# Summing w_out from its bf16 tile instead of its f32 load buffers, in a fused attention and MLP kernel

## The chip, the cores and the metric

The kernel runs on one core of a Trainium2 chip. The metric is device time in microseconds of one launch, as the median of several runs. A core has a tensor engine (PE) for matrix products, a vector engine (DVE), a scalar engine for activations (ACT), a general engine (POOL), and a sync engine (SP), which here issues nearly all the transfers (DMA). Each engine works through its own list of instructions in order; engines wait for each other by semaphores. A profile of one execution stands beside the times.

## The reference

Attention with 4 sequences, 8 heads, 768 tokens and 64 elements a head, each query seeing the 8 first keys and the 96 latest ones, with a distance bias; then softplus between two weight products.

```python
scores = scale * np.matmul(q, k.transpose(0, 1, 3, 2))
...
scores = scores + bias[None, :, :, :]
scores = np.where(keep, scores, -1000000000.0)
...
a = a / (np.sum(a, axis=-1, keepdims=True) + 1e-09)
return np.matmul(a, v).astype(np.float32)
...
h = x @ w_in
g = np.maximum(h, 0.0) + np.log1p(np.exp(-np.abs(h)))
return (g @ w_out).astype(np.float32)
```

x is the attention's output with its heads put side by side (3072 tokens of 512). w_in is 512 x 2048, w_out 2048 x 512.

## The kernel before, in words

**Tiling.** The 3072 tokens are 24 blocks of 128 (numbered n = 0 to 23 in the order of `UNITS`), two blocks a load unit (i = 0 to 11) and two blocks a group (g = 0 to 11) for the weight products.

**One block's attention.** q, k and v of a unit are loaded in f32 (`ldq`, `ldk`, `ldv`, lines 598 to 644, 512 KB each) into a ring of 14 buffers called raw; cast to bf16 (`castq`, `castk`, `castv`); q and k are transposed, from unit 3 on by DMA (`trq`, `trk`, lines 853 to 868). Then scores on PE (`sc`, line 980), bias added on DVE (`z`, line 1006), exponentials on ACT (`ex`, line 1013), the weighted values on PE (`pv`, line 1032), the normalizing on DVE (`nm`, lines 1043 and 1044), and a transpose to the tile XT (`xt`, line 1075, by DMA). The copies `gk` and `gv` bring the 8 global keys and values into the rows that the block before no longer needs, so they wait for that block's `pv`.

**One group's weight products.** `a{g}.{p}` is the first product in eight parts of eight matmuls (line 1227), `e` the exponential (line 1255) and `ln` the logarithm (line 1265) that make softplus; the result is the tile g. For groups 0 and 1 the second product is dense: `b{g}.{half}.{x}` (line 1286), two matmuls of 512 columns each, then a copy `oc` and a store. From group 2 on the second product is made by seven block products instead of eight (Strassen): `b{g}.{j}`, j from 1 to 7, eight matmuls of 256 columns each (line 544). Five of them multiply with sums or differences of quarters of w_out, and five with differences of quarters of g (`ka`, line 468). `oe` puts the products together in the output tile (lines 499 to 527). Groups 10 and 11 make the first product by seven block products too (`kw`, `kx`, `mA` to `mD`, `mt`, `md`, `eo`, `ed`).

**w_out and its sums.** `wout0` to `wout7` (line 669) load 256 rows each, 512 KB, into raw buffers. `cout0` to `cout7` (line 673) cast them into the bf16 tile `w_out_bf`, which groups 0 and 1 and the products 2 and 5 use. `weight_sums` (lines 409 to 441) makes twenty sums of 128 x 512, `ws{p}.{j}` (line 430): for each p from 0 to 3 and each j of 6, 1, 4, 3, 7, from the rows of `wout{2p}` (X) and `wout{2p+1}` (Y); j = 6 needs X alone and j = 7 needs Y alone. They go to DVE or POOL, in bf16, into raw buffers that have become free (`homes`, among them those of w_out 0, 1 and 2). The buffers of w_out 3, 4 and 5 return to the ring at the end of `weight_sums`, and by the ring's order they are the next homes of `ldk4`, `ldv4` and `ldq5`.

**The order.** All steps stand in one list, `ORDER`, written out by hand, each with its engine (P for PE, V for DVE, A for ACT, G for POOL, S for SP); each engine issues its steps in the order of the list. A step's waits follow from what it reads and writes (`Program.op`, lines 28 to 54). Loads from unit 3 on are also gated by a part of the first product (lines 1517 to 1521), so that they do not come too early: for `ldk3` that is `a0.4`. Up to some 28 us PE also has 35 fillers (`fill`, line 1414), products of a blank tile that keep its clock up.

```python
op(f"ws{p}.{j}", "DVE", 0.0, rank, ex, reads={"6": xk, "7": yk}.get(j, xk + yk), writes=[("W", j, p)],
   port=True, after=[u for key in raw_keys(slot, (part // 2,)) for u in users(key)],
   alts={"DVE": 0.66, "POOL": 1.3})
...
for slot in (at[6], at[7]):
...
idle.extend((at[3], at[4], at[5]))
```

Of the kernel before, what the change touches and what calls it, by code (L numbers as in the profile page):

```python
# [85 lines left out]
castq2.1:V a0.3:P e0.0:A gk8:G ldv2:S castk2.1:V xt2:P ln0.0:A trq2.0:P xc2:V trk2.0:P e0.3:A wout3:S cin5:V pv3.0:P  # L86
fill32:P cpk2.1:A a0.2:P nm3.0:V cin4:V fill33:P e0.2:A pv3.1:P fill34:P cpq2.1:V a0.5:P gv8.1:G ln0.1:A cpk2.0:V
nm3.1:V cin6:G a0.4:P e0.5:A cpq2.0:V wout4:S xt3:P e0.4:A cin7:V sc4.0:P xc3:V ln0.2:A a0.7:P wout5:S z4.0:V cout0:G
a0.6:P e0.7:A z4.1:V ldq3:S b0.0.0:P e0.6:A cout1:G a1.1:P ws0.4:V ex4.1:A ldk3:S a1.0:P ws0.3:V e1.1:A b0.0.2:P
cout2:V e1.0:A a1.3:P wout7:S ex4.0:A ws0.1:V castv2.00:G a1.2:P castv2.01:V ln1.0:A gk5:G b0.0.4:P ws0.6:V pv4.0:P  # L90
e1.2:A sc5.0:P ws1.4:V e1.3:A b1.0.0:P nm4.0:V cout3:A b1.0.2:P ws2.6:G a1.5:P z5.0:V ln0.3:A pv4.1:P wout6:S cout4:G
b0.0.6:P nm4.1:V ldv3:S sc5.1:P e1.5:A gv5.0:V a1.4:P cout5:A castv2.10:G z5.1:V castv2.11:G xt4:P castq3.0:A a1.7:P
ws1.7:V gv5.1:G ws1.1:V b0.1.0:P e1.4:A trq3:S b0.1.2:P ln1.1:A b0.1.4:P ws0.7:V b0.0.8:P xc4:A castk3.0:V b0.1.6:P
ex5.0:A a1.6:P ws2.7:V ws1.3:V e1.7:A ldq4:S b0.1.8:P cout6:V ex5.1:A b0.1.10:P trk3.0:S b0.0.10:P cout7:V b1.0.4:P
e1.6:A ws2.1:V pv5.0:P gk6:A b0.1.12:P ln1.2:A ldk4:S nm5.0:V b0.0.12:P trk3.1:S ws2.4:V b0.0.14:P pv5.1:P ws2.3:V
oc0.0.0:A b0.1.14:P gv6.0:G b1.0.6:P ln1.3:A nm5.1:V b1.0.8:P ldv4:S oc0.1.0:V castv3.11:G b1.0.10:P castq4.0:A
gv6.1:V xt5:P castv3.00:G sc6.0:P xc5:V castv3.10:A castv3.01:G trq4:S b1.0.12:P z6.0:V b1.0.14:P ws1.6:G a2.1:P
oc1.0.0:A ldq5:S z6.1:V ex6.0:A a2.0:P castk4.0:G ex6.1:A pv6.0:P b1.1.0:P trk4.0:S nm6.0:V b1.1.2:P e2.0:A gk7:V
pv6.1:P ws3.3:V e2.1:A sc7.0:P gv7.1:G nm6.1:V ln2.0:A ldk5:S a2.2:P z7.0:V gv7.0:G xt6:S a2.3:P castv4.10:G e2.2:A
z7.1:V ex7.0:A ws3.4:G b1.1.4:P b1.1.6:P trk4.1:S e2.3:A gv8.0:V b1.1.8:P castq5.0:G pv7.0:P ex7.1:A sc8.0:P nm7.0:V  # L100
st0.0.0:S a2.5:P ln2.1:A z8.0:V trq5:S castv4.01:G castv4.11:G pv7.1:P e2.5:A b1.1.10:P nm7.1:V castv4.00:G a2.4:P
ex8.0:A z8.1:V xt7:S a2.7:P e2.4:A ws3.6:V ex8.1:A st0.1.0:S pv8.0:P b1.1.12:P nm8.0:V ldv5:S a2.6:P e2.7:A ldq6:S
ws3.7:V gk9:G ln2.2:A b1.1.14:P pv8.1:P castk5.0:G oc1.1.0:V sc9.0:P e2.6:A ws3.1:V a3.1:P ln2.3:A trk5.0:S gv9.1:G
z9.0:V a3.0:P e3.1:A gv9.0:G ldk6:S b2.3:P z9.1:V ka2.6:G e3.0:A ex9.0:A b2.4:P nm8.1:V ex9.1:A ka2.7:V a3.2:P xt8:S
pv9.0:P e3.2:A gk10:G a3.3:P nm9.0:V ldv6:S oe2.a:A trk5.1:S ka2.2:V a3.4:P e3.3:A ka2.1:V ln3.0:A pv9.1:P sc10.0:P
nm9.1:V gv10.0:G e3.4:A a3.5:P z10.1:V xt9:S castq6.0:G b2.1:P e3.5:A ka2.5:V ldq7:S ex10.1:A a3.6:P oe2.1:V trq6:S
gv10.1:V a3.7:P z10.0:V gk11:G e3.6:A castv5.00:G ln3.1:A b2.5:P castv5.01:G castk6.0:V st1.0.0:S e3.7:A b2.2:P
castv6.01:G ldk7:S ex10.0:A trk6.0:S sc11.0:P oe2.c:V castv5.11:G a4.0:P z11.1:V castq7.0:G trk6.1:S pv10.0:P e4.0:A
b2.7:P nm10.0:V ln3.3:A castv5.10:G z11.0:V a4.2:P trq7:S castv6.11:G ln3.2:A pv10.1:P a4.1:P st1.1.0:S gv11.0:G
e4.2:A ka3.6:V b2.6:P gv11.1:G e4.1:A nm10.1:V ex11.0:A a4.4:P ka3.2:V castv6.00:G xt10:S oe2.7:V a4.3:P e4.4:A  # L110
castk7.0:G ldv7:S sc12.0:P e4.3:A pv11.0:P z12.1:V b3.3:P trk7.0:S ka3.1:G ex11.1:A nm11.0:V a4.5:P ln4.0:A z12.0:V
pv11.1:P e4.5:A a4.6:P nm11.1:V ex12.0:A castv6.10:V xt11:S b3.4:P ex12.1:A ka3.7:V e4.6:A a4.7:P ka3.5:G oe3.a:V
ln4.1:A st2.0.0:S sc13.0:P ldq8:S e4.7:A ldv9:S pv12.0:P z13.1:V b3.1:P ln4.3:A ldk8:S a5.0:P castv7.00:V ex13.1:A
oe3.1:V a5.1:P ldv8:S z13.0:V castv7.01:A gk14:G b3.5:P e5.0:A nm12.0:V e5.1:A b3.2:P ex13.0:A trk7.1:S castq8.0:G
sc14.0:P oe3.c:V ln4.2:A castv7.11:G pv12.1:P a5.2:P nm12.1:V castv9.00:G ln5.0:A z14.1:V a5.3:P castv7.10:G xt12:S
pv13.0:P castv9.10:G castv9.11:V e5.3:A b3.7:P castk8.0:G ex14.1:A st2.1.0:S nm13.0:V b3.6:P ka4.1:V gk15:A trk8.0:S
a5.5:P e5.2:A castv8.11:G oe3.7:V ln5.1:A pv13.1:P castv8.01:G a5.4:P st3.0.0:S nm13.1:V gv14.1:G z14.0:V xt13:S
b4.3:P e5.4:A e5.5:A b4.4:P ka4.7:V ldq9:S ln5.2:A ka4.5:V a5.6:P trq8:S castv9.01:V gv14.0:A a5.7:P ka4.6:V oe4.a:A
st3.1.0:S kw1.1:V e5.6:A ka4.2:G sc15.0:P e5.7:A b4.1:P ex14.0:A a6.0:P trk8.1:S oe4.1:V z15.1:V a6.1:P e6.0:A ldk9:S
ln5.3:A pv14.0:P ldv10:S b4.5:P nm14.0:V castq9.0:G ex15.1:A z15.0:V b4.2:P ldk11:S ka5.6:G gk16:A pv14.1:P e6.1:A  # L120
oe4.c:V a6.2:P trq9:S ex15.0:A nm14.1:V sc16.0:P gv15.1:A a6.3:P gv15.0:G z16.0:V castk9.0:G b4.7:P e6.3:A z16.1:V
e6.2:A pv15.0:P castv8.00:G trk9.1:S b4.6:P ln6.0:A nm15.0:V castv8.10:G a6.5:P oe4.7:V ex16.1:A castv10.10:G ka5.1:V
a6.4:P st4.0.0:S ex16.0:A xt14:S pv15.1:P b5.3:P gk17:A gv16.1:V e6.5:A gv16.0:V nm15.1:V ldq10:S b5.4:P ka5.2:V
trk9.0:S pv16.0:P ka5.7:V oe5.a:A sc17.0:P nm16.0:V e6.4:A xt15:S ka5.5:G b5.1:P z17.0:V ln6.2:A pv16.1:P a6.6:P
st4.1.0:S gv17.1:A oe5.1:V ldv11:S a6.7:P gv17.0:V e6.6:A nm16.1:V ex17.0:A z17.1:V b5.5:P xt16:S castk11.0:G e6.7:A
b5.2:P ldk10:S ln6.3:A pv17.0:P oe5.c:V sc18.0:P ln6.1:A a7.1:P z18.1:V castq10.0:V a7.0:P ex18.1:A nm17.0:V e7.1:A
b5.7:P z18.0:V e7.0:A ex18.0:A b5.6:P ka6.1:V ex17.1:A a7.2:P castk10.0:G oe5.7:V ka6.7:V sc19.0:P st5.0.0:S e7.2:A
castv10.11:G st5.1.0:S a7.3:P ln7.0:A z19.0:V trq10:S ka6.5:G pv17.1:P e7.3:A b6.3:P nm17.1:V ex19.0:A trk10.0:S
z19.1:V a7.4:P castv11.11:G pv18.0:P xt17:S b6.4:P e7.4:A nm18.0:V castv10.00:G kw1.0:V a7.5:P oe6.a:A castv11.10:G
trk10.1:S pv18.1:P a7.6:P e7.5:A nm18.1:V castv10.01:G ex19.1:A kw5.0:V b6.1:P ldq11:S e7.6:A a7.7:P gk20:G oe6.1:V  # L130
ka6.6:V a8.0:P e7.7:A ka6.2:V ln7.3:A pv19.0:P a8.1:P nm19.0:V ln7.1:A kw5.1:V b6.5:P kw7.0:V e8.0:A pv19.1:P kw7.1:V
b6.2:P e8.1:A castv11.01:V ln7.2:A a8.2:P oe6.c:V sc20.0:P e8.2:A ka7.6:G a8.3:P ln8.0:A z20.1:V b6.7:P e8.3:A
nm19.1:V ex20.1:A castv11.00:G a8.4:P z20.0:V xt19:S gv20.1:G b6.6:P gk21:A e8.4:A ka7.2:V gv20.0:G xt18:S ex20.0:A
a8.5:P oe6.7:V castq11.0:G ka7.7:V sc21.0:P st6.1.0:S e8.5:A trk11.0:S a8.6:P ln8.1:A z21.0:V ka7.5:G pv20.0:P e8.6:A
b7.3:P st6.0.0:S trk11.1:S nm20.0:V ex21.0:A a8.7:P z21.1:V b7.4:P trq11:S e8.7:A kw2.0:V ex21.1:A a9.0:P ka7.1:V
pv20.1:P oe7.a:V gk22:G e9.0:A a9.1:P gv21.1:G nm20.1:V ln8.2:A b7.1:P kw6.1:V xt20:S e9.1:A gv21.0:V a9.2:P oe7.1:V
ln8.3:A kw6.0:V pv21.0:P sc22.0:P e9.2:A ka8.6:G nm21.0:V ln9.0:A a9.3:P z22.1:V pv21.1:P e9.3:A a9.4:P z22.0:V
ex22.1:A gv22.1:G b7.5:P gv22.0:V e9.4:A nm21.1:V a9.5:P ex22.0:A gk23:V xt21:S ka8.2:V b7.2:P e9.5:A kw2.1:V ln9.1:A
sc23.0:P oe7.c:V a9.6:P z23.0:V ln9.2:A kx10.1:G a9.7:P e9.6:A z23.1:V kx10.3:G pv22.0:P e9.7:A b7.7:P kx10.7:G
nm22.0:V ln9.3:A kx10.4:G mA10.0:P ka8.1:V b7.6:P kx10.6:G my10.0:A mA10.1:P oe7.7:V mA10.3:P my10.1:A mA10.2:P  # L140
pv22.1:P my10.2:A mB10.0:P st7.0.0:S nm22.1:V ex23.0:A gv23.0:G mB10.1:P st7.1.0:S mt10.0:V mB10.2:P gv23.1:G xt22:S
ex23.1:A b8.3:P mt10.1:V ka8.7:G pv23.0:P mC10.0:P nm23.0:V b8.4:P mt10.2:V eo10.0:A ka8.5:G pv23.1:P oe8.a:A mC10.1:P
nm23.1:V mD10.0:P eo10.1:A xt23:S b8.1:P md10.0:V mC10.2:P my10.3:A ka9.6:G oe8.1:V mD10.1:P eo10.2:A mB10.3:P b8.5:P
# [1431 lines left out]
```

## Time and profile before

| what | us |
|---|---|
| median of 3 runs (lowest, highest) | 210.27 (209.87, 211.12) |
| the profiled execution's own time | 210.3 |
| its span, from the first to the last instruction | 208.5 |
| PE busy | 200.5 |
| DVE busy | 175.5 |
| ACT busy | 165.9 |
| POOL busy | 109.2 |

Busy time is a sum over the whole span; it does not say which engine sets the end. For that the profile follows the chain that ended last, back from the last instruction: at each step to what released it, or to the instruction before it on its engine. PE has 93% of that chain. A group of instructions is shown as line, engine, operation, tiles and shapes, then its count, busy time, mean time of one in ns, and the idle time ahead of it with what ended it. A timeline row is its start, its duration, the engine, the line and the tiles. The granted clock was 0.998 of the full one.

### The profile page before, as it was taken

The numbers are of one execution on the slowest core, as the hardware profiler recorded it, in microseconds if no ns is written. First come the engines' busy times: TensorE is split into PE (matmuls) and PEld (weight loads), VectorE is DVE, ScalarE is ACT, GpSimd is POOL, SyncE is SP. The second block draws the span as 40 slices with busy tenths as digits, with TensorE's granted clock in tenths as the row PEclk, the third lists the DMA queues.
The fourth block names the chain that finished last, engine by engine and source line by source line (L and its number), as shares of the span: only waits on it lengthen the run. The fifth ranks groups of instructions, "written<-read, shape, count | busy, mean of one in ns | idle before, by whom it ended". The sixth has DMA issues, their size and how long they took to land.

```text
span 208.5 us, 5775 instructions
## 1 busy us (share of the span) xinstructions
PE 200.5 (96%) x2307; PEld 165.0 (79%) x2307; DVE 175.5 (84%) x330; ACT 165.9 (80%) x245; POOL 109.2 (52%) x130
## 2 busy tenths in 40 slices
...
GB/s 174 364 360 389 386 356 362 335 236 266 190 250 214 245 207 306 200 177 305 215 198 271 219 220 214 186 145 0 119 161 14 16 129 28 101 3 101 0 63 143
DMA packets 70650, 41.00 MB, mean 197 GB/s; under 512 B 30432, under 2 KB 62688, under 8 KB 70624
## 3 DMA queue, kind: packets, MB, share of 16 engines
...
q10 hardware_dynamic: 688, 0.66, 1.0%
...
## 4 chain that ended last, share of the span: by engine, by line
PE 93%; DMA 3%; DVE 1%; ACTq 0%; ACT 0%; POOL 0%; issue 0%; DVEq 0%
PE h_ps L1227 34%; PE o_ps L544 27%; PE s_ps L980 6%; PE x_ps L1032 5%; PE o_ps L1286 3%; PE s_ps L1286 3%; PE h_ps L1167 3%; DMA raw<-in_q_dram 3%; PE s_ps L1167 3%; PE x_ps L1414 2%; PE s_ps L544 1%; PE s_ps L840 1%; PE x_ps L544 1%; PE o_ps L1032 1%; PE s_ps L961 1%; PE s_ps L820 0%
## 5 line engine op out<-in xcount | busy, mean ns | idle before, releaser
L1227 PE MATMUL h_ps<-XT,w_in_bf 128*128 128x256 bf16 x640 | 79.6, 273 | 0.0
L1227 PEld LDWEIGHTS <-w_in_bf 128*128 128x128 bf16 x640 | 60.5, 98 | 9.8
L1255 ACT ACTIVATE e<-h_ps 128x512 f32<-128x512 f32 x80 | 50.1, 640 | 9.3 <-PE h_ps L1227 8.8
L1006 DVE TENSOR_TENSOR z<-s_ps,biasA 128x1024 f32<-128x1024 f32 x38 | 45.6, 1216 | 1.9 <-PE s_ps L980 1.9
L1013 ACT ACTIVATE pb<-z 128x1024 bf16<-128x1024 f32 (+1 forms) x44 | 43.1, 992 | 0.7 <-DVE rcp L1043 0.4
L1265 ACT ACTIVATE g<-e 128x1024 bf16<-128x1024 f32 x40 | 41.7, 1054 | 0.4
L544 PEld LDWEIGHTS <-g 128*128 128x128 bf16 x320 | 30.6, 98 | 3.8 <-issue 0.5
L468 POOL TENSOR_TENSOR raw<-g 128x1024 bf16<-128x1024 bf16 x10 | 21.3, 2132 | 14.2 <-PE o_ps L544 5.6
L544 PE MATMUL o_ps<-raw,raw 128*128 128x256 bf16 x224 | 28.2, 273 | 0.0
L736 POOL CAST vb<-raw 64x512 bf16<-64x512 f32 x35 | 24.3, 699 | 6.2 <-DMA raw<-in_v_dram 4.9
L544 PEld LDWEIGHTS <-raw 128*128 128x128 bf16 x240 | 22.7, 98 | 2.7
L898 POOL COPY vb<-vb 4x512 bf16<-4x512 bf16 x19 | 13.0, 683 | 22.6 <-PE x_ps L1032 17.9
L1032 PEld LDWEIGHTS <-pb 128*128 128x128 bf16 x352 | 16.5, 98 | 3.5 <-ACT pb L1013 0.6
L544 PE MATMUL o_ps<-w_out_bf,g 128*128 128x256 bf16 x152 | 18.5, 273 | 0.4 <-DVE osb L502 0.4
L1044 DVE TENSOR_TENSOR xs<-x_ps,rcp 128x256 bf16<-128x256 f32 x40 | 17.0, 425 | 1.4
L468 POOL TENSOR_TENSOR g<-g 128x1024 bf16<-128x1024 bf16 x6 | 13.1, 2178 | 9.7 <-DVE raw L468 5.6
L544 PE MATMUL o_ps<-raw,g 128*128 128x256 bf16 x144 | 17.8, 273 | 0.0
L468 DVE TENSOR_TENSOR raw<-g 128x1024 bf16<-128x1024 bf16 x20 | 16.5, 823 | 1.0 <-ACT g L1265 0.6
L1032 PE MATMUL x_ps<-vb,pb 128*128 128x65 bf16 x304 | 15.8, 193 | 0.0
L1414 PE MATMUL x_ps<-blank 128*128 128x512 bf16 x35 | 12.0, 465 | 1.2 <-DVE blank L1338 1.2
L716 POOL CAST kb<-raw 128x1024 bf16<-128x1024 f32 x7 | 7.3, 1038 | 9.3 <-DMA raw<-in_k_dram 6.9
L1043 DVE RECIPROCAL rcp<-x_ps 128x4 f32<-128x4 f32 x40 | 7.1, 177 | 4.2 <-PE x_ps L1032 3.2
(150 smaller groups left out, 285.1 us busy)
## 6 DMA issues: line engine op xcount, KB each, us to landing
...
```

Source lines behind the costliest of these rows:

```text
L468: (nc.vector if eng == "DVE" else nc.gpsimd).tensor_tensor(dst, a[0], b[0], ALU.subtract)
L544: nc.tensor.matmul(psum(j), lhs[:, f // 2, f % 2, :], w(f), start=(f == 0 and not (chain and j in ("67" if g in APART else "267"))), stop= ...
L736: copy_on[eng](dst, src)
L898: copy_on[eng](vb_of(prev)[sl, :, 0:D], vb_of(first)[sl, :, 0:D])
L1006: nc.vector.tensor_tensor(z, src, bias, ALU.add)
L1013: nc.scalar.activation(pb[:, 0:nr, :].rearrange("p (y a) b -> p y (a b)", y=2), src, AF.Exp, scale=1.0 / root_d)
L1032: nc.tensor.matmul(xv[:, h, :], pb[:, 4 * (h % 2) + 2 * part + h // 2 if lone else u_all * (2 * (h % 2) + h // 2) + u, :], vb_of(prev if u ...
L1044: nc.vector.tensor_tensor(xs[:, 4 * part : 4 * part + 4, :], xv[:, :, 0:D], rcp[:][:, :, None].to_broadcast([P, 4, D]), ALU.mult,)
L1227: last = nc.tensor.matmul(hv[:, j, :], w_in_bf[:, m, fb * P : fb * P + P], XT[g % NXG][:, m, :], start=(m == 0), stop=(m == NM - 1),)
L1255: nc.scalar.activation(e[:, p % 2, :, :].rearrange("p j (b t r) -> p (j b) r t", b=2, r=2), hb[:].rearrange("p (a r t) -> p a r t", a=4, r=2),
L1265: nc.scalar.activation(gt[:, 2 * p - 2 : 2 * p + 2, :].rearrange("p a t -> p (a t)"), e[:].rearrange("p a j t -> p (a j t)"), AF.Ln, bias=1.0,
L1414: nc.tensor.matmul(x_ps[:], blank[:, 0:P], blank[:])
```

## The change

Two things change. In `weight_sums` X and Y are no longer views of the f32 load buffers but of the bf16 tile `w_out_bf`, and the keys by which a sum waits are those of the casts (`("wout", 2p)` and `("wout", 2p + 1)`) instead of those of the loads. So a sum stands behind the cast of the rows that it reads, and a load buffer of w_out is free when it has been cast. And `ORDER` is a new list from its fourteenth line on: the same 1097 steps, 109 of them on another engine; PE has the same 341 and SP the same 126, DVE has 266 instead of 270, ACT 249 instead of 242, POOL 115 instead of 118.

```diff
-            X, Y = (raw_t[at[x]][:].rearrange("p (a c) -> p a c", a=2) for x in (2 * p, 2 * p + 1))
-            xk, yk = raw_keys(at[2 * p]), raw_keys(at[2 * p + 1])
+            X, Y = (w_out_bf[:, 2 * x : 2 * x + 2, :] for x in (2 * p, 2 * p + 1))
+            xk, yk = [("wout", 2 * p)], [("wout", 2 * p + 1)]
```

Where the sums are made:

| engine | before | after |
|---|---|---|
| DVE | 17 | 13 (0.1, 0.4, 0.6, 0.7, 1.3, 1.4, 1.6, 1.7, 2.3, 2.4, 2.7, 3.1, 3.6) |
| POOL | 3 (1.6, 2.6, 3.4) | 7 (0.3, 1.1, 2.1, 2.6, 3.3, 3.4, 3.7) |

The parts of the two lists that the prediction speaks of, engine by engine:

```diff
 PE, around the scores of blocks 4, 6 and 8
-a0.5 a0.4 xt3 sc4.0 a0.7 a0.6 b0.0.0 a1.1 a1.0
+a0.5 a0.4 sc4.0 xt3 a0.6 a0.7 b0.0.0 a1.0 a1.1
...
-pv5.1 b0.1.14 b1.0.6 b1.0.8 b1.0.10 xt5 sc6.0
+b0.1.14 b1.0.4 b1.0.6 pv5.1 b1.0.8 sc6.0 xt5 b1.0.10
...
-sc7.0 a2.2 a2.3 b1.1.4 b1.1.6 b1.1.8 pv7.0 sc8.0 a2.5
+sc7.0 a2.3 pv6.1 a2.2 b1.1.4 a2.5 pv7.0 sc8.0 b1.1.6
 SP
-wout3 wout4 wout5 ldq3 ldk3 wout7 wout6 ldv3 trq3 ldq4 trk3.0 ldk4 trk3.1 ldv4 trq4 ldq5 trk4.0 ldk5 xt6 trk4.1
+wout3 ldk3 wout4 wout6 wout5 ldq3 wout7 ldv3 trk3.0 trk3.1 trq3 ldq4 ldk4 ldv4 ldq5 trq4 trk4.0 ldk5 trk4.1 xt6
 DVE
-ws0.4 ws0.3 cout2 ws0.1 castv2.01 ws0.6 ws1.4 nm4.0 z5.0 nm4.1 gv5.0 z5.1 ws1.7 ws1.1 ws0.7 castk3.0
+cout1 cout2 z5.0 ws1.6 cout3 z5.1 ws1.7 nm4.0 ws1.3 nm4.1 castv2.11 gv5.0 ws2.4 ws1.4 castq3.0 ws0.1 ws0.4 ws3.6 cout7 nm5.0
 POOL
-cout0 cout1 castv2.00 gk5 ws2.6 cout4 castv2.10 castv2.11 gv5.1 gv6.0 castv3.11 castv3.00 castv3.01 ws1.6 castk4.0
+cout0 gk5 castv2.01 ws1.1 cout4 cout6 cout5 gk6 ws3.3 castv3.11 gv6.1 gv6.0 castv3.10 castq4.0 castv3.00 castk4.0
...
-ka9.6 kx11.3 ka9.7 kx11.6 ka10.6 ka10.7
+ka9.6 kx11.6 ka9.2 kx11.3 ka9.7 kx11.7 ka9.5 ka10.6 ka10.2 ka10.1
```

More of the change, by code (lines that the diff above doesn't have):

```diff
@@ L85 @@
 fill28:P fill29:P wout0:S fill30:P cin2:G e0.1:A fill31:P pv2.1:P a0.0:P wout1:S ex3.1:A nm2.1:V castq2.0:G wout2:S
[L86 to L143, printed above, removed]
-mt10.3:V b8.2:P kx11.3:G md10.1:V kx11.1:V mC10.3:P oe8.c:V mD10.2:P eo10.3:A kx11.7:V mA11.0:P kx11.4:V b8.7:P
@@ L145 @@
-md10.2:V my11.0:A ed10.0:A ka9.2:V b8.6:P ka9.1:V mD10.3:P oe8.7:V ka9.7:G mA11.1:P mA11.2:P md10.3:V mB11.0:P
-st8.0.0:S b9.3:P st8.1.0:S my11.2:A mt11.0:V b9.4:P my11.1:V kx11.6:G mB11.2:P oe9.a:A mC11.0:P mt11.2:V ed10.1:A
-b9.1:P eo11.0:A ka9.5:V mC11.2:P ed10.2:A oe9.1:V mA11.3:P mB11.1:P ed10.3:A b9.5:P mt11.1:V eo11.2:A ka10.6:G b9.2:P
-mD11.2:P oe9.c:V mD11.0:P md11.2:V b9.7:P md11.0:V b9.6:P ka10.2:V my11.3:A ed11.2:A mB11.3:P oe9.7:V ka10.7:G
-mC11.1:P mt11.3:V st9.0.0:S b10.3:P eo11.1:A st9.1.0:S ka10.1:V b10.4:P mD11.1:P ka10.5:V oe10.a:A mC11.3:P md11.1:V
@@ L150 @@
-b10.1:P eo11.3:A ed11.0:A mD11.3:P oe10.1:V ed11.1:A md11.3:V b10.5:P ed11.3:A b10.2:P b11.3:P oe10.c:V ka11.6:V
-b10.7:P ka11.2:V b10.6:P ka11.1:V b11.4:P ka11.7:V oe10.7:V b11.1:P oe11.a:A ka11.5:V st10.1.0:S b11.2:P oe11.1:V
-b11.5:P oe11.2:V st11.1.0:S b11.6:P st10.0.0:S oe11.5:V b11.7:P oe11.6:V st11.1.1:S st11.0.1:S oe11.7:V st11.0.0:A
+castq2.1:V a0.3:P e0.0:A ldv2:S castk2.1:V xt2:P ln0.0:A gk8:V trq2.0:P xc2:V trk2.0:P cpq2.1:A wout3:S cin5:V pv3.0:P
+fill32:P e0.3:A a0.2:P nm3.0:V cpk2.0:A cpq2.0:V fill33:P cpk2.1:A cin4:V fill34:P pv3.1:P e0.2:A a0.5:P gv8.1:V
@@ new lines @@
+gv8.0:G nm3.1:V ln0.1:A cin6:G a0.4:P sc4.0:P cin7:V ldk3:S e0.4:A xt3:P e0.5:A z4.0:V a0.6:P ln0.2:A cout0:G wout4:S
+a0.7:P xc3:V z4.1:V e0.6:A b0.0.0:P e0.7:A a1.0:P cout1:V ex4.1:A a1.1:P cout2:V e1.0:A wout6:S gk5:G b0.0.2:P wout5:S
+e1.1:A sc5.0:P ldq3:S ln1.0:A b0.0.4:P z5.0:V castv2.01:G a1.2:P ex4.0:A wout7:S ws1.6:V a1.3:P cout3:V sc5.1:P e1.3:A
+ws1.1:G b1.0.0:P z5.1:V ldv3:S castv2.00:A b1.0.2:P e1.2:A a1.5:P ws1.7:V castk3.0:A pv4.0:P a1.4:P cout4:G nm4.0:V
+ln0.3:A trk3.0:S ws1.3:V b0.1.0:P b0.1.2:P e1.4:A cout6:G pv4.1:P b0.0.6:P gv5.1:A nm4.1:V b0.0.8:P castv2.10:A
```

61 lines of the change are left out of this document (added).

## The prediction

> **What bounds the kernel now.** I read the busy times by stretch first, then the chain that ended last, then the few waits that the chain shows on the tensor engine (PE). The stretches are cut where the work changes: up to 28 us the first loads, to 67 us the dense output products of groups 0 and 1 with the sums of w_out, to 166 us the steady part, then the end.
>
> ```profile
> 28.00:67.00 39.00, 38.31 (x408) 27.29 (x408) 35.63 (x61) 36.62 (x49) 21.30 (x29) 1.00 1.16 270
> 67.00:166.00 99.00, 99.00 (x1183) 86.73 (x1182) 88.82 (x153) 89.78 (x129) 58.49 (x66) 1.00 0.84 182
> 166.00:208.50 42.50, 38.02 (x471) 35.00 (x468) 30.45 (x60) 17.64 (x30) 15.70 (x11) 0.99 0.22 70
> ```
>
> The columns are the stretch, its length, busy PE, PE's weight loads, DVE, ACT, POOL, the granted clock, the DMA share and GB/s. PE is idle for 0.69 us between 28 and 67 us and not at all between 67 and 166 us, at full clock. The twenty sums lie in the first of these stretches, on DVE and POOL. PE's busy ends are modelled, so I check it with the chain, which has the pieces one behind the other.
>
> ```profile
> 26.05 1.75 PE h_ps L1227 x16
> ...
> 47.03 0.24 PE x_ps L1032 x8
> 47.27 0.43 PE s_ps L1286 x2
> ...
> 49.22 0.55 PE s_ps L980 x16
> ...
> 54.61 1.85 PE h_ps L1227 x16
> ...
> 57.76 0.26 PE x_ps L1032 x8
> ...
> 58.03 0.20 DVE rcp L1043
> ...
> 58.25 0.44 DVE xs L1044
> 58.69 0.61 PE s_ps L980 x16
> ```
>
> A 256-column matmul takes 1.75/16 = 0.109 us and a 512-column one 0.43/2 = 0.215 us, the same 0.42 ns a column, and each piece starts where the last one ends. There is one hole: the weighted values pv7.0 end at 57.76 + 0.26 = 58.02 and the scores sc8.0 start at 58.69, 0.67 us later. A second one lies at the end.
>
> ```profile
> 192.87 0.89 PE o_ps L544 x8
> ...
> 193.84 0.70 DVE osb L502
> ...
> 194.58 1.91 PE L544 MATMUL o_ps<-w_out_bf,g 128*128 128x256 bf16 x16 [0.39 <-DVE osb L502]
> ```
>
> b10.1 ends at 193.76 and b10.5 starts at 194.58; mD11.3 lies between, and PE idles 0.39 us. PE's work is the same 341 steps in both orders, with the same 35 fillers, and the order is unchanged up to about 23 us, so all that can be gained behind that is these two holes, 0.67 + 0.39 = 1.06 us, 0.5%. What can be lost has no such limit.
>
> **The first hole** looks like a wait for DVE, but the weight load in front of it names another:
>
> ```profile
> 58.67 0.10 PEld L980 LDWEIGHTS <-kT 64*128 64x128 bf16 x2 [0.80 <-DMA kT<-kb]
> 51.70 0.53 SPq L638 DMA_DIRECT2D raw<-in_q_dram  x1
> 52.49 2.30 SPq L860 DMA_TRANSPOSE kT<-kb  x1
> DMA to landing us min/median/max: 6.1/6.1/6.1
> ```
>
> The last line is that of the transpose issued at 52.49, trk4.0. It lands at 52.49 + 6.1 = 58.6, and sc8.0 needs it. Just ahead of it SP had sent ldq5, a 512 KB load, at 51.70.
>
> **The change, part by part.** (1) The instructions. Twenty sums of 512 elements read bf16 instead of f32.
>
> ```profile
> L430 DVE TENSOR_TENSOR raw<-raw,raw 128x512 bf16<-128x512 f32 x11 | 7.7, 714 | 0.0
> L468 DVE TENSOR_TENSOR g<-g 128x1024 bf16<-128x1024 bf16 x14 | 9.9, 708 | 0.1
> L1131 DVE TENSOR_TENSOR kb<-XT 128x256 bf16<-128x256 bf16 x2 | 0.6, 285 | 0.0
> L430 POOL TENSOR_TENSOR raw<-raw 128x512 bf16<-128x512 f32 x2 | 2.5, 1274 | 1.9 <-DMA raw<-in_moe_w_out_dram 1.8
> L468 POOL TENSOR_TENSOR raw<-g 128x1024 bf16<-128x1024 bf16 x10 | 21.3, 2132 | 14.2 <-PE o_ps L544 5.6 <-ACT g L1265 5.1 <-ACT g L1179 3.3
> L1131 POOL TENSOR_TENSOR qb<-XT 128x256 bf16<-128x256 bf16 x5 | 3.2, 675 | 3.5 <-DMA XT<-xs 3.5
> ```
>
> No bf16 sum of 512 stands in the trace. On DVE it lies between 0.285 us (256 elements) and 0.71 us (1024); on the line through both it is 0.285 + (0.708 - 0.285)/3 = 0.43, which I take. On POOL the line gives 0.675 + (2.132 - 0.675)/3 = 1.16, between 0.68 and 2.13. The new order has 13 sums on DVE and 7 on POOL, the old 17 and 3. DVE: 17 x 0.71 = 12.1 us becomes 13 x 0.43 = 5.6 (3.7 to 9.2). POOL: 3 x 1.28 = 3.8 becomes 7 x 1.16 = 8.1 (4.8 to 14.9). So DVE gets some 6 us and POOL loses some 4 in 39. In the time this counts as nothing: PE runs through beside them. The cover is PE's row; gone, at the far ends, it is POOL's 11 us more, against its 39 - 21.3 = 17.7 us idle.
>
> (2) The slots. The load buffers of w_out 3, 4 and 5 are the next homes of ldk4, ldv4 and ldq5. These no longer wait for sums, only for casts. In the new order all of ldq4, ldk4, ldv4, ldq5 stand ahead of trq4; in the old one ldq5 stood between trq4 and trk4.0.
>
> (3) sc8.0, as I work it out. Ahead of sc8.0 the new order lacks b1.1.6 and b1.1.8 (0.86 us) and has a2.5 (0.87) more: it is due at 58.02 again. castk4.0 is on POOL behind gv6.1, gv6.0, castv3.10, castq4.0, castv3.00, and the gv copies wait for pv5.1, which has b0.1.14 and b1.0.6 more ahead of it (2 x 0.43): 47.03 + 0.86 + 0.24 = 48.13.
>
> ```profile
> L736 POOL CAST vb<-raw 64x512 bf16<-64x512 f32 x35 | 24.3, 699 | 6.2 <-DMA raw<-in_v_dram 4.9
> L898 POOL COPY vb<-vb 4x512 bf16<-4x512 bf16 x19 | 13.0, 683 | 22.6 <-PE x_ps L1032 17.9 <-PE o_ps L1032 4.3
> L716 POOL CAST kb<-raw 128x1024 bf16<-128x1024 f32 x7 | 7.3, 1038 | 9.3 <-DMA raw<-in_k_dram 6.9
> kT<-kb SPq DMA_TRANSPOSE x14, 4.1
> ```
>
> 2 x 0.68 + 2 x 0.70 + 2 x 1.04 = 4.8, so castk4.0 ends at 53.0 and trk4.0 goes out at 53.1 to 53.5, as SP may still be issuing trq4. Only trq4 is ahead of it, as ldq5 left some 5 us before. At the median 4.1 us it lands by 57.6, in time. The old 6.1 would make it 59.6, 1.6 us late (0.9 more than now); I take 4.1, because the load that went ahead is gone. Gain 0.67, bounds -0.9 to +0.67.
>
> (4) The added wait. ws2.4 on DVE now waits for the cast cout5. Behind it stand ws1.4, castq3.0, ws0.1, ws0.4, ws3.6, cout7 and nm5.0; trq3 waits for castq3.0, and sc6.0 for trq3. On SP ldk3 moves ahead of w_out 4, 6, 5, then ldq3, w_out 7, ldv3.
>
> ```profile
> L669 SPq DMA_DIRECT2D raw<-in_moe_w_out_dram x1: 2802/2802/2802, 23.2 to 23.2; - x1
> DMA to landing us min/median/max: 11.3/11.3/11.3
> ...
> 30.69 2.74 SPq L638 DMA_DIRECT2D raw<-in_k_dram  x1
> DMA to landing us min/median/max: 10.0/10.0/10.0
> L669 SPq DMA_DIRECT2D raw<-in_moe_w_out_dram x1: 3452/3452/3452, 33.5 to 33.5; - x1
> DMA to landing us min/median/max: 8.8/8.8/8.8
> 40.65 2.80 SPq L867 DMA_TRANSPOSE qT<-qb  x1
> DMA to landing us min/median/max: 5.6/5.6/5.6
> ```
>
> The fourth load behind w_out 3 lands at 30.7 + 10.0 = 40.7, the fifth at 33.5 + 8.8 = 42.3. Now these places are those of w_out 5 and q3. ldk3 is gated by the product a0.4, which ends at 26.05 + 1.75 = 27.8 us, so SP stands until then; w_out 3 lands only at 23.2 + 11.3 = 34.5, so the DMA engines have work meanwhile, and I cost this at nothing (without that backlog, 2 us). cout5 then ends at 40.7 + 1.04 = 41.8 and ws2.4 goes at about 42; castq3.0 comes two sums later, and at L468's 0.71 for as many elements it ends at 42 + 2 x 0.43 + 0.71 = 43.6; trq3 lands between 43.6 + 4.1 = 47.7 (kT's median) and 43.6 + 5.6 = 49.2. sc6.0 is due at 49.22 less b1.0.10 and xt5 (0.65), which now come later: 48.6. So 0 to 0.6 us; I take 0, as the old trq3, 3 us earlier, had w_out 7, w_out 6 and v3 still ahead of it in the queue (the first of them landed at 42.3), and the new one hardly more than v3.
>
> (5) The rest of the order: 109 steps change engine. I compared, for each product that reuses a PSUM bank, the PE work between it and the last user of the bank. One cover shrinks to its need: a0.4 to a0.6 has sc4.0 and xt3 between, 0.77 us (1.64 before), and e0.4, which must be done, took 28.48 - 27.80 = 0.68. I take nothing, bounds 0 to 0.2. On ACT, cout3, cout5, castq3.0 and castq4.0 leave this stretch and castk3.0, three more castv and two gv come, of 1.04 and some 0.6 us each on POOL's rows: the sum stays near. At the end POOL takes ka9.2, ka9.5, ka10.2 and ka10.1.
>
> ```profile
> 27.83 0.65 ACT L1255 ACTIVATE e<-h_ps 128x512 f32<-128x512 f32 x1 [0.17 <-PE h_ps L1227]
> ...
> 178.98 2.14 POOL L468 TENSOR_TENSOR raw<-g 128x1024 bf16<-128x1024 bf16 x1 [3.37 <-PE o_ps L544]
> 184.86 1.75 PE o_ps L544 x16
> ```
>
> ka9.7 waits for b8.6, now 0.22 later: 179.2. With kx11.7 and ka9.5 behind it, 2.13 + 0.68 + 2.13, ka9.5 is done at 184.1, 0.7 us ahead of b9.5 at 184.86; ka10.6, ka10.2 and ka10.1, 3 x 2.13, by 190.5, ahead of b10.1 at 192.87. The hole of 0.39 us stays, since between b10.1 and b10.5 still stands mD11.3 alone.
>
> Sum: profiled time 210.3 (span 208.5 and 1.8 around it; the median of the runs is 210.27) - 0.67 = **209.6**.
>
> **The rivals.** *No change*: DMA and not the order of the queue sets trk4.0, the hole stays: 210.3. For it: the DMA share of 1.16 in that stretch.
>
> *Slower, at sc6.0*: the gate in ldk3 empties the DMA queue, w_out 5 and q3 slip by 2 us, DVE waits in ws2.4, trq3 lands at 47.7 + 2 to 49.2 + 2; at the later end sc6.0 starts 2.6 us late: 209.6 + 2.6 = 212.2. It decides when trq3 lands after 48.6. Against it: the 34.5.
>
> *Slower, in the steady part*: DVE and ACT have 10% idle there, and a step behind a late one on its engine holds PE. I found none, but did not follow all moves; two or three holes of 0.7 us cost 1.4 to 2.1: 211.0 to 211.7.
>
> *Faster*: PE's matmuls are stretched by waits and have more to give. The 16 behind scores take 1.85 instead of 1.75; 0.1 at each of 24 blocks is 2.4 us: 207.2 at the least. Against it: 0.42 ns a column at both widths.
> The Trainium skill, Perfetto Trace Analysis, "Identifying the Most-Contended Engine", calls matmul busy time a bad measure of the limit and takes the weight loads' share instead. Here that is 27.29/39.00 = 70%, which by that rule leaves PE nearly 12 us in this stretch; the columns speak against it.
>
> **How the numbers follow.** Forecast 0.47, no change 0.15, slower in the steady part 0.22, slower at sc6.0 0.08, faster 0.08. A measurement of this kernel can tell about 0.5%, 1.05 us, from no change: below 209.2 and above 211.3. Faster: 0.08 and 0.04 of the forecast's lower side (both holes gone), 0.12. Slower: 0.08, 0.16 of the 0.22, and 0.04 of the forecast's upper side (trk4.0 at 6.1 with sc6.0 late too): 0.28. Same: the rest, 0.60. The range 209.0 to 212.2 leaves out the faster case and the worst of the slower ones.
>
> **What would show it.** Right: no hole at sc8.0, trk4.0 landing about 4 us from its issue, ldq5 issued near 46 us, DVE's sums near 0.43 us, the hole before b10.5 as before. Wrong: a hole in front of sc6.0, DVE idle at a sum behind POOL's cast, or PE idle between 67 and 166 us.

## The result, and the profile after

The changed kernel takes 213.39 us (median of 6 runs, 212.76 to 214.39) against 210.26 (6 runs, 209.64 to 211.12): a ratio of 1.0149, interval 1.0116 to 1.0182. It is 3.1 us slower; the forecast was 209.6, and 213.39 lies above the range. The profiled execution took 213.37 us with a span of 211.3. Lines of the new kernel are numbered one higher (sums 431, `ka` 469, `castv` 737).

The busy time by stretch, columns as before:

```profile
28.00:67.00 39.00, 38.20 (x403) 27.18 (x404) 33.47 (x55) 36.71 (x53) 23.23 (x29) 1.00 1.12 264
67.00:166.00 99.00, 96.99 (x1151) 83.55 (x1148) 89.04 (x153) 91.06 (x125) 60.02 (x61) 1.00 0.88 184
166.00:211.30 45.30, 41.05 (x505) 37.66 (x502) 32.57 (x66) 20.57 (x34) 21.49 (x15) 0.99 0.20 65
```

PE now idles 2.0 us in the steady part, where it idled not at all. DVE, ACT and POOL are no busier there than before by more than 1.6 us, so no engine has become the bound; the clock is full. The chain that ended last says the same, by engine on the page, and then in order of time where it leaves PE:

```profile
PE 68%; DVE 13%; DMA 6%; issue 4%; POOL 3%; SPq 2%; ACT 2%; ACTq 0%; DVEq 0%; POOLq 0%
```
```profile
118.66 1.76 PE o_ps L545 x16
...
120.44 0.69 DVE osb L500
121.13 0.03 issue
121.16 0.21 DVE vb L737
121.38 2.08 issue
123.46 1.22 DVE z L1007
...
125.14 0.69 DVE osb L503
125.83 0.04 issue
125.88 1.14 PE o_ps L545 x9
```

PE had 93% of the chain and has 68%. The piece to look at is "issue 2.08" behind a cast on DVE: DVE waits for nothing that the chain can name. The timeline of DVE, and that of POOL, show what it is:

```profile
121.16 2.26 DVE L737 CAST vb<-raw 64x512 bf16<-64x512 f32 x1
123.46 1.22 DVE L1007 TENSOR_TENSOR z<-s_ps,biasA 128x1024 f32<-128x1024 f32 x1
...
125.14 0.68 DVE L503 TENSOR_TENSOR osb<-osb,o_ps 128x512 f32<-128x512 f32 x1
```
```profile
121.02 2.12 POOL L469 TENSOR_TENSOR g<-g 128x1024 bf16<-128x1024 bf16 x1
123.09 0.80 POOL L737 CAST vb<-raw 64x512 bf16<-64x512 f32 x1
```

The cast castv9.01 takes 2.26 us; it starts 0.14 us after POOL's ka5.5 and ends, at 123.42, 0.28 us after ka5.5 does, at 123.14. Behind it on DVE stand z17.0, nm16.0 and oe5.1 (the row at 125.14). PE's pv16.1 needs nm16.0 and waits 1.36 us for it, and b5.5 behind pv16.1 needs oe5.1:

```profile
125.28 0.40 PE L1033 MATMUL x_ps<-vb,pb 128*128 128x65 bf16 x8 [1.36 <-DVE xs L1045]
125.88 1.91 PE L545 MATMUL o_ps<-w_out_bf,g 128*128 128x256 bf16 x16 [0.19 <-DVE osb L503]
```

In the kernel before, the same cast on DVE stood beside no POOL instruction, and the scores sc18.0 came without a wait:

```profile
104.74 0.42 DVE L736 CAST vb<-raw 64x512 bf16<-64x512 f32 x1
```

So 1.84 us of the cast are a hold, that is, time in which the instruction has started and does not get on. They are counted as busy: no view by busy time shows them. A second place of the chain is a wait for a load, with three casts and two `ka` behind it on POOL:

```profile
82.91 5.93 DMA raw<-in_v_dram
...
88.96 0.61 POOL vb L737
...
90.91 2.10 POOL raw L469
93.00 0.07 issue
93.07 2.14 POOL g L469
95.22 0.05 issue
95.26 1.05 PE o_ps L545 x8
```

castv7.01 heads POOL's queue until the load of v7 lands; ka3.6 and ka3.2 do not need that load, but stand behind it, and b3.2 at 95.26 needs ka3.2.

The sums themselves came out as estimated. Groups by line:

```profile
L431 DVE TENSOR_TENSOR raw<-w_out_bf 128x512 bf16<-128x512 bf16 x13 | 9.3, 734 | 0.0
L431 POOL TENSOR_TENSOR raw<-w_out_bf 128x512 bf16<-128x512 bf16 x7 | 8.0, 1153 | 5.2 <-DMA raw<-in_v_dram 3.3 <-DVE w_out_bf L674 1.9
```

POOL's take 1.153 us. DVE's mean of 0.734 hides two kinds: eleven of 0.41 or 0.42 and two that were held, ws0.7 and ws2.7 (DVE, then POOL beside the first):

```profile
52.44 2.31 DVE L431 TENSOR_TENSOR raw<-w_out_bf 128x512 bf16<-128x512 bf16 x1
62.05 2.71 DVE L431 TENSOR_TENSOR raw<-w_out_bf 128x512 bf16<-128x512 bf16 x1
```
```profile
52.31 1.04 POOL L717 CAST kb<-raw 128x1024 bf16<-128x1024 f32 x1
53.31 1.15 POOL L431 TENSOR_TENSOR raw<-w_out_bf 128x512 bf16<-128x512 bf16 x1
```

ws0.7 lasts through two POOL instructions and ends at 54.75, 0.29 us after the second.

### The profile page after: what moved, and what is told of

Its sections match the earlier page's. It is cut to its first block, busy times and chain, and to the rows that moved or that the text cites. A ratio compares the mean times of both kernels' runs of the same rounds, so it can differ in the third digit from the quotient of the medians.

```text
span 211.3 us, 5748 instructions
## 1 busy us (share of the span) xinstructions
PE 201.0 (95%) x2297; PEld 164.3 (78%) x2307; DVE 176.0 (83%) x326; ACT 170.6 (81%) x250; POOL 117.9 (56%) x129
## 4 chain that ended last, share of the span: by engine, by line
PE 68%; DVE 13%; DMA 6%; issue 4%; POOL 3%; SPq 2%; ACT 2%; ACTq 0%; DVEq 0%; POOLq 0%
PE o_ps L545 22%; PE h_ps L1228 22%; DVE z L1007 5%; PE s_ps L981 4%; PE x_ps L1033 3%; PE s_ps L1287 3%; DMA raw<-in_v_dram 3%; DMA raw<-in_q_dram 3%; PE s_ps L1168 3%; PE h_ps L1168 2%; PE x_ps L1415 2%; PE o_ps L1287 2%; PE s_ps L545 1%; SPq L861 1%; DVE xs L1045 1%
## 5 line engine op out<-in xcount | busy, mean ns | idle before, releaser
L1228 PEld LDWEIGHTS <-w_in_bf 128*128 128x128 bf16 x640 | 59.9, 98 | 9.7 <-DVE w_in_bf L674 0.3
L1256 ACT ACTIVATE e<-h_ps 128x512 f32<-128x512 f32 x80 | 49.2, 633 | 4.9 <-PE h_ps L1228 4.3
L469 POOL TENSOR_TENSOR g<-g 128x1024 bf16<-128x1024 bf16 x12 | 26.0, 2171 | 18.2 <-DVE raw L469 14.6
L899 POOL COPY vb<-vb 4x512 bf16<-4x512 bf16 x19 | 12.5, 659 | 21.0 <-PE x_ps L1033 12.8
L469 POOL TENSOR_TENSOR raw<-g 128x1024 bf16<-128x1024 bf16 x8 | 17.4, 2179 | 6.8 <-ACT g L1266 3.6
L737 POOL CAST vb<-raw 64x512 bf16<-64x512 f32 x21 | 14.2, 674 | 8.5 <-DMA raw<-in_v_dram 7.7
L469 DVE TENSOR_TENSOR raw<-g 128x1024 bf16<-128x1024 bf16 x22 | 15.6, 718 | 0.7 <-PE o_ps L545 0.5
L1415 PE MATMUL x_ps<-blank 128*128 128x512 bf16 x32 | 10.9, 467 | 1.2 <-DVE blank L1339 1.2
L431 POOL TENSOR_TENSOR raw<-w_out_bf 128x512 bf16<-128x512 bf16 x7 | 8.0, 1153 | 5.2 <-DMA raw<-in_v_dram 3.3
```

Source lines behind the costliest of these rows:

```text
L469: (nc.vector if eng == "DVE" else nc.gpsimd).tensor_tensor(dst, a[0], b[0], ALU.subtract)
L737: copy_on[eng](dst, src)
L899: copy_on[eng](vb_of(prev)[sl, :, 0:D], vb_of(first)[sl, :, 0:D])
L1228: last = nc.tensor.matmul(hv[:, j, :], w_in_bf[:, m, fb * P : fb * P + P], XT[g % NXG][:, m, :], start=(m == 0), stop=(m == NM - 1),)
L1256: nc.scalar.activation(e[:, p % 2, :, :].rearrange("p j (b t r) -> p (j b) r t", b=2, r=2), hb[:].rearrange("p (a r t) -> p a r t", a=4, r=2),
L1415: nc.tensor.matmul(x_ps[:], blank[:, 0:P], blank[:])
```

## The experiments

**Theory**: the sums from bf16 cost nothing and bring nothing; the new order costs 3.1 us at a few places where a step that PE needs stands on DVE, ACT or POOL behind one that is held up, most of it by a hold of DVE beside POOL. **Rival**: the change of operands costs (the wait for the casts), or the gain at sc8.0 exists and something larger hides it. Ratios are to the kernel before.

**1. The operands alone**, in the old order; two sums that would have stood ahead of their casts go behind them.

```diff
 DVE
-castv2.01 ws0.6 ws1.4 nm4.0 z5.0
+castv2.01 ws0.6 nm4.0 ws1.4 z5.0
 POOL
-gk5 ws2.6 cout4
+gk5 cout4 ws2.6
```

> The order of before with the sums read from the bf16 tile; only ws1.4 and ws2.6 move, each just behind the cast it now needs. My theory (the loss is in the new order's steady part, not in the operands): 210.3 us as before, within 0.4. Rival (the bf16 sums or their waits for the casts cost the time themselves): 1.5 us or more above before, 211.8 to 213.4.

Measured: 210.55, ratio 1.0024 (1.0000 to 1.0048). Stretch to 67 us:

```profile
28.00:67.00 39.00, 38.46 (x409) 27.53 (x404) 30.97 (x62) 36.50 (x49) 21.14 (x29) 1.00 1.17 271
```

DVE has 4.7 us less to do than before (35.63) and the time does not fall. It rises by 0.2%, at the edge of what is measured: ws1.4 now heads DVE's queue until its cast on ACT is done, 1.00 us, and z5.0, which PE's scores sc5.1 need, stands behind it; they wait 0.44 us for it.

```profile
36.99 0.43 DVE L430 TENSOR_TENSOR raw<-w_out_bf 128x512 bf16<-128x512 bf16 x1 [1.00 <-ACT w_out_bf L673]
```

So nearly all of the 3.1 us came in with the order. The new order with the sums still from f32 was not run.

**2. castv9.01 on ACT** in the new order, and **3. ka3.6 and ka3.2 ahead of castv7.01** on POOL.

```diff
 DVE (2)
-ka5.1 oe5.a castv9.01 z17.0
+ka5.1 oe5.a z17.0
 ACT (2)
-castv10.00 ln6.2
+castv10.00 castv9.01 ln6.2
 POOL (3)
-castq7.0 castv7.01 castv7.10 castv7.00 ka3.6 ka3.2 castk8.0
+castq7.0 ka3.6 ka3.2 castv7.01 castv7.10 castv7.00 castk8.0
```

> The changed kernel with one step on another engine: castv9.01 on ACT instead of DVE. My theory (this cast takes 2.26 us on DVE because POOL's ka5.5 runs beside it, and PE waits 1.86 us at b5.5 and b5.2 for the steps queued behind the cast): 213.4 - 1.9 = 211.5 us. Rival (the hole before b5.5 is set by something else, and ACT only gets one more cast): 213.4 or a little above.

> The changed kernel with ka3.6 and ka3.2 put ahead of castv7.01, castv7.10 and castv7.00 in POOL's list. My theory (b3.2 starts 0.5 to 0.6 us late because POOL stands at castv7.01 until the load v7 lands at 88.8 us): 213.4 - 0.5 = 212.9 us, and no hole before b3.2. Rival (the four us that the casts come later cost as much elsewhere): 213.4 or above.

Measured: 211.47, ratio 1.0055 (1.0029 to 1.0080), so 1.9 us off for one cast, as expected; and 213.09, ratio 1.0127 (1.0090 to 1.0163), 0.3 us off for an expected 0.5.

**4. Both, and castv8.10 on POOL** instead of ACT.

```diff
 ACT
-e5.4 castv8.10 e5.5
+e5.4 e5.5
 POOL
-gv14.0 gk15
+gv14.0 castv8.10 gk15
```

> The changed kernel with three moves: castv9.01 on ACT, ka3.6 and ka3.2 ahead of the castv7 casts on POOL, and castv8.10 on POOL instead of ACT (oe4.a stands behind it on ACT, and b4.1 starts 0.4 us late). My theory (three places hold the whole loss): 213.4 - 1.9 - 0.5 - 0.3 = 210.7 us. Rival (the new order is slower in many small places, or the holes reappear elsewhere): above 212.

Measured: 211.30, ratio 1.0035 (1.0015 to 1.0056), 2.1 us off and not 2.7, between the theory and its rival: what sc15.0 gains, the product a6.1 behind it loses again.

**5. All sums on DVE.** The seven POOL sums move to DVE at their places in the list.

```diff
-ws0.3:G ws1.1:G ws2.1:G ws2.6:G ws3.3:G ws3.4:G ws3.7:G
+ws0.3:V ws1.1:V ws2.1:V ws2.6:V ws3.3:V ws3.4:V ws3.7:V
```

> The new order with all seven POOL sums (0.3, 1.1, 2.1, 2.6, 3.3, 3.4, 3.7) made on DVE at the same places of the list, 20 on DVE and none on POOL. Theory A (DVE instructions with all their operands in SBUF stand until POOL's instruction, or a run of them, has ended): ws0.7 (2.31 us) and ws2.7 (2.71 us) come down to at most one POOL cast's length, 0.4 to 1.5 us, the hole of 0.4 us ahead of pv7.0 goes, the later holes stay: 0.3 to 0.5 us below the changed kernel, 212.9 to 213.1. Theory B (what DVE is given is what costs): 7 x 0.41 = 2.9 us more on DVE in the stretch to 67 us, at least as slow as the changed kernel, 213.4 or more.

Measured: 213.7, ratio 1.0141 (1.0099 to 1.0183): no change, and not the 0.3 to 0.5 us less that were expected. The long holds did go (the first row is ws0.7 with ws3.7 behind it, 1.17 and 0.83 us; ws0.7 now ends 0.28 us after the one cast beside it), but the hole ahead of pv7.0 stayed, at 0.31 us, and its weight load names ACT:

```profile
52.52 1.92 DVE L431 TENSOR_TENSOR raw<-w_out_bf 128x512 bf16<-128x512 bf16 x2
```
```profile
58.06 0.29 PEld L1033 LDWEIGHTS <-pb 128*128 128x128 bf16 x8 [0.31 <-ACT pb L1014]
```

So that part of the theory fell: the stretch from sc7.0 to sc8.0 shortens by 0.15 us (table below), and the rest of the hole at pv7.0 is not the sum's. On ACT the copy gv7.1, which POOL made before, stands ahead of ex7.0, the maker of pb:

```profile
56.30 0.62 ACT L899 COPY vb<-vb 4x512 bf16<-4x512 bf16 x1
56.95 2.01 ACT L1014 ACTIVATE pb<-z 128x1024 bf16<-128x1024 f32 x2
```

**6. ldq5 behind trk4.0** in the old order, sums from f32.

```diff
 SP
-trq4 ldq5 trk4.0 ldk5
+trq4 trk4.0 ldq5 ldk5
```

> The kernel before, its sums still from the f32 rows, with one step moved: on SP the 512 KB load ldq5 is issued behind the transpose trk4.0 instead of ahead of it. If trk4.0 was late because of the load ahead of it in the queue, it lands some 4 us from its issue instead of 6.1, sc8.0 has no hole, and the time falls by 0.5 to 0.7 us to 209.6 to 209.8. Rival (the transpose takes 6 us by itself in that stretch): the hole of 0.67 us stays, 210.3. If castq5.0 then waits for the later load, a new hole of up to 1 us stands ahead of sc10.0.

Measured: 210.57, ratio 0.9999 (0.9976 to 1.0021). trk4.0 landed 3.7 us from its issue, sc8.0 came at 57.82 with no hole, and the time stayed. In this profile most of the gain is given back within 8 us: ws3.6, a sum from f32 that takes 0.68 us alone, now starts beside POOL, which has a cast, two small copies and a cast in a row, and takes 2.22 us. nm8.0 stands behind it, and pv8.1 waits 0.50 us. It is the hold that castv9.01 shows, in the old order.

```profile
61.39 2.22 DVE L430 TENSOR_TENSOR raw<-raw 128x512 bf16<-128x512 f32 x1
64.22 0.28 PEld L1032 LDWEIGHTS <-pb 128*128 128x128 bf16 x7 [0.50 <-issue]
```

**7. ka5.5 on DVE**, behind castv9.01, which stays where it was.

```diff
 DVE
-oe5.a castv9.01 z17.0
+oe5.a castv9.01 ka5.5 z17.0
 POOL
-castv9.11 ka5.5 castv9.00
+castv9.11 castv9.00
```

> The new order with one step on another engine: ka5.5 on DVE, right behind castv9.01, instead of on POOL beside it. castv9.01 stays where it is. Theory A (POOL's instruction holds it): castv9.01 takes 0.43 us instead of 2.26, ka5.5 0.7, oe5.1 ends some 1.1 us earlier and the holes of 1.86 us ahead of b5.5 and b5.2 shrink to 0.7 or less: 1.1 to 1.9 us below the changed kernel, 211.5 to 212.3. Theory B (the cast waits for its load or for another event): castv9.01 still ends near 123.4, ka5.5 comes on top, 213.4 to 214.1.

Measured: 212.36, ratio 1.0078 (1.0045 to 1.0111), 1.0 us off. DVE and POOL:

```profile
121.30 0.71 DVE L737 CAST vb<-raw 64x512 bf16<-64x512 f32 x1
122.04 0.69 DVE L469 TENSOR_TENSOR g<-g 128x1024 bf16<-128x1024 bf16 x1
```
```profile
120.46 1.26 POOL L737 CAST vb<-raw 64x512 bf16<-64x512 f32 x2
```

The same cast, from the same load, takes 0.71 us: it ends at 122.01, 0.29 us after POOL's casts at 121.72. What it waited for was POOL's instruction; this decides against a wait for data.

**8. Five edits**: those of 2, 3 and 5, and gv8.1 later on DVE (in the new order it took 1.34 us beside POOL's gv8.0 and a cast, and PE's weight load at 29.09 waited 0.28 us for a cast of w_in on DVE; here it takes 0.29).

```diff
 DVE
-cpq2.0 cin4 gv8.1 nm3.1
+cpq2.0 cin4 nm3.1
...
-nm5.0 oc0.1.0
+nm5.0 gv8.1 oc0.1.0
```

> The new order with the steps that were found late put elsewhere, all together: castv9.01 on ACT, ka3.6 and ka3.2 ahead of castv7.01 on POOL, gv8.1 on DVE behind nm5.0 (some 20 us later, away from POOL's copy), all twenty sums on DVE. castv8.10 stays on ACT. Theory A: 1.9 + 0.3 + 0.4 (ahead of pv7.0) + 0.4 (ahead of sc5.0) = 3.0 us below the changed kernel, 210.4, level with the kernel before; what is left is the holes at 106 us (0.3 to 0.5) and 172 us (0.25) less the hole at sc8.0 that is gone. Theory B (the holes are given back elsewhere, by whatever step is late next): 211.3 or more, as with three fixes.

Measured: 210.77, ratio 1.0013 (0.9992 to 1.0035), 2.6 us off for an expected 3.0.

**9. Eight edits**: gv7.1 to POOL behind gv7.0, castv8.10 to POOL as in 4, and

```diff
 DVE
-ka4.1 ka4.2 z14.0 ka4.7
+ka4.1 z14.0 ka4.2 ka4.7
```

> The new order with the five edits of the kernel before this one (castv9.01 on ACT, ka3.6 and ka3.2 ahead of castv7.01, gv8.1 later, all twenty sums on DVE) and three more: gv7.1 on POOL instead of ACT, castv8.10 on POOL instead of ACT, ka4.2 behind z14.0 on DVE. Theory: the hole ahead of pv7.0 came from ACT, where gv7.1 (0.62 us) stood ahead of ex7.0, and not from the sum ws0.7, so it goes now: -0.3 to -0.4; and the hole at 106 us came from oe4.a and ex14.0 behind castv8.10 and z14.0: -0.3 to -0.5. That gives 209.9 to 210.1 against 210.77 with five edits, 0.2% below the kernel before. Rival: PE ahead by that much only waits for the transposes instead (a4.0 had 0.36 us of such a wait already): 210.4 to 210.8.

Measured: 210.61, ratio 1.0008 (0.9987 to 1.0030), in the rival's range and not in the theory's. The hole at pv7.0 is gone with gv7.1; the wait for transposes ahead of a4.0 stands:

```profile
57.47 0.39 PEld L1033 LDWEIGHTS <-pb 128*128 128x128 bf16 x8
...
80.32 1.64 PEld L1228 LDWEIGHTS <-w_in_bf 128*128 128x128 bf16 x16 [0.38 <-DMA XT<-xs]
```

**10. The operands and ldq5 ahead of trq4**, old order; the edit of run 1, and

```diff
 SP
-trq4 ldq5 trk4.0
+ldq5 trq4 trk4.0
```

> The old order with the sums from the bf16 tile and one step moved: on SP the load ldq5 goes ahead of trq4, which it can, since its buffer is free as soon as it has been cast. Theory (the load ahead of trk4.0 made the hole at sc8.0): trk4.0 lands some 4 us from its issue, the hole goes, PE is 0.3 to 0.7 us ahead at 60 us, and if that lasts the time is 209.6 to 210.0. Rival (what is gained at sc8.0 is given back, because the steps behind it, sc9.0 and later the transposes at 107 and 126 us, were due only when they were): 210.3 to 210.6.

Measured: 211.01, ratio 1.0029 (1.0001 to 1.0058): slower, if anything. sc8.0 has no hole; but ws1.4 behind its cast was also held, 1.27 us, and sc5.1 waited 1.29; and the transpose kTa ahead of sc18.0 was late by 1.20 us.

```profile
37.25 1.27 DVE L430 TENSOR_TENSOR raw<-w_out_bf 128x512 bf16<-128x512 bf16 x1 [1.00 <-ACT w_out_bf L673]
```
```profile
127.02 0.23 PEld L980 LDWEIGHTS <-kTa 64*128 64x128 bf16 x8 [1.20 <-DMA kTa<-kb]
```

**11 and 12. Both kernels, unchanged, profiled a second time.**

> The kernel before, unchanged, profiled a second time: how much of a profile is the execution's own. If the holes are the program's, the one of 0.67 us ahead of sc8.0 is there again within 0.1 us and there is none ahead of sc18.0 (125 us). If they hang on when DMAs land in one execution, the first moves by some tenths and a hole of 0.4 to 1.2 us may stand ahead of sc18.0, as in the three kernels made from the old order; then what was gained at sc8.0 in them was not given back there by the edit.

> The changed kernel, unchanged, profiled a second time. If its holes are the program's, those ahead of pv7.0 (0.4 us), b3.2 (0.6 us) and b5.5 with b5.2 (1.6 and 0.27 us) are there again within 0.1 us, and castv9.01 takes over 2 us again; if they hang on DMAs they move by several tenths.

Measured: 209.75 (span 208.0) and 213.5 (span 211.6). In the second profile of the kernel before there is no hole at sc8.0: pv7.0's load starts at 57.33 and that of sc8.0 at 57.87, without a wait. trk4.0 was issued at nearly the same time, 52.42 instead of 52.49, and landed 5.3 us later, not 6.1. Run 1, with the same list for SP, has 5.3 and no hole either. So the hole stands in one of three profiles in which ldq5 goes out just ahead of trk4.0; in the other eleven, where it does not, trk4.0 lands in 3.7 to 4.9 us. Ahead of sc18.0 the old kernel has no hole in either profile; those of 0.41, 0.68 and 1.20 us there belong to runs 6, 1 and 10, and whether the edits or the executions made them is not decided.

```profile
57.33 0.49 PEld L1032 LDWEIGHTS <-pb 128*128 128x128 bf16 x8
57.87 0.10 PEld L980 LDWEIGHTS <-kT 64*128 64x128 bf16 x2
```
```profile
kT<-kb SPq DMA_TRANSPOSE x1, 5.3
```

The changed kernel's holes were all there again. Since PE has the same list in runs 2 to 5, 7 to 9 and 12, its timeline can be cut at the same steps in all of them. From the start of one step's first weight load to that of the next, in us, the stretches that differ:

| from, to | after | 12 again | 2 | 3 | 4 | 5 | 7 | 8 | 9 |
|---|---|---|---|---|---|---|---|---|---|
| a0.5, sc5.0 | 7.51 | 7.51 | 7.51 | 7.51 | 7.51 | 7.51 | 7.51 | 7.11 | 7.11 |
| sc7.0, sc8.0 | 4.56 | 4.55 | 4.55 | 4.55 | 4.55 | 4.40 | 4.55 | 4.40 | 4.20 |
| sc10.0, a4.0 | 9.99 | 10.43 | 10.23 | 9.97 | 10.10 | 11.12 | 10.15 | 10.26 | 10.35 |
| sc13.0, b3.2 | 7.30 | 7.49 | 7.50 | 6.70 | 6.70 | 7.27 | 7.22 | 6.70 | 6.70 |
| b4.1, sc15.0 | 1.35 | 1.34 | 1.33 | 1.33 | 1.07 | 1.32 | 1.32 | 1.33 | 1.07 |
| sc15.0, a6.3 | 2.86 | 2.71 | 2.71 | 2.98 | 3.23 | 2.71 | 2.72 | 2.85 | 3.15 |
| sc17.0, b5.5 | 5.16 | 5.16 | 3.64 | 5.16 | 3.64 | 5.16 | 4.21 | 3.64 | 3.65 |
| b5.5, sc18.0 | 3.09 | 3.09 | 2.74 | 3.09 | 2.74 | 3.09 | 3.09 | 2.74 | 2.74 |

All other stretches up to the last product agree within 0.13 us. Five of the eight have their wait in an engine's queue: unedited, they repeat to 0.03 us. The other three move by themselves: that to a4.0, which a transpose can end, has 9.99 and 10.43 us in the same kernel and 9.97 to 11.12 in all; that to b3.2, which the load of v7 can end, 7.22 to 7.50; and that to a6.3 has 2.86 and 2.71 in the same kernel. From the first column to the last the eight edits take 0.40 + 0.36 + 0.60 + 0.28 + 1.51 + 0.35 = 3.50 us, give back 0.29 at a6.3 and, with the wait at a4.0, 0.36: 2.85, against 213.39 - 210.61 = 2.78 in the medians. The kernel before was 0.3 us slower in run 9's rounds than in the first ones (210.60 and 210.26), so the ratio is the better measure of what is left: 0.08%, or 0.2 us, which its interval does not tell from nothing. The loss is so accounted for, with the sums still made from bf16. What stays untested is a wait of 0.25 us ahead of mA10.3 near 172 us. No version beats the kernel before.

## Why the prediction was wrong

The case that came is its rival "slower, in the steady part", with 0.22, but larger than it was priced, and with 0.76 of its 3.50 us ahead of the steady part, at sc5.0 and pv7.0.

- **(1) The instructions** were right: 0.41 us on DVE and 1.15 on POOL, for 0.43 and 1.16. That they count as nothing is what run 1 shows, with 4.7 us less on DVE, but for the wait at sc5.1 in the old order. In the new order DVE's busy time fell by only 2.2 us in that stretch, as the holds of ws0.7 and ws2.7 put 1.9 and 2.3 us back.
- **(2) The slots** were right: ldq5 (the first row below) goes ahead of trq4.
- **(3) sc8.0** was worked out rightly for the new order and wrongly for the old. trk4.0 was to go out at 53.1 to 53.5 and land by 57.6; it went out at 53.37 (SP's timeline of the changed kernel, the second row), landed 4.4 us later, and sc8.0 followed pv7.0 without a wait. But the term of 0.67 us in the sum was not a gain to count on: the second profile of the old kernel does not have the hole. One execution's late transpose was taken for a property of the program. The rival "no change" is not borne out in its reason, since trk4.0 does land sooner with ldq5 elsewhere (3.7 to 4.9 us, not 5.3 to 6.1); only that this brings no time is so, by run 6.

```profile
47.06 2.58 SPq L639 DMA_DIRECT2D raw<-in_q_dram  x1
...
53.37 1.92 SPq L861 DMA_TRANSPOSE kT<-kb  x1
```

- **(4) The added wait** at sc6.0 was right: no hole there. The wait is real where nothing covers it, as ws1.4 in runs 1 and 10.
- **(5) The rest of the order is the step that failed.** The prediction put the 109 moved steps at nothing. It said "I compared, for each product that reuses a PSUM bank, the PE work between it and the last user of the bank", and for ACT "the sum stays near". That covers one kind of lateness, and of the steady part it said itself that it "did not follow all moves". The time went to three other kinds: a step held beside another engine's (castv9.01, 1.51 + 0.35 us; gv8.1, 0.40; the held sums, 0.15), a step behind a load on a queue (ka3.2 behind castv7.01, 0.60), and a step that changed engine and went ahead of one that PE needs (gv7.1 on ACT, 0.20; castv8.10, 0.28, moved rather than removed by its edit).
- **The price of the rival**, "two or three holes of 0.7 us", was an estimate from the one hole in view. The largest loss, 1.51 + 0.35 = 1.86 us, comes from one cast, whose 2.26 us go through z17.0, nm16.0 and oe5.1 to PE. PE's 99.00 of 99.00 busy us in the steady part only said that the old order had no late step there; it was no cover for a new one.
